# Gated linear attention and a maxout feed-forward: two groups of tokens ahead of most of the weight rounding

## The chip, the cores and the metric

The kernel runs on one core of a Trainium2 chip. The metric is the device time of one execution in microseconds. The core's engines work side by side, each through its own list of instructions in order: TensorE (PE, with its weight loads PEld), VectorE (DVE), ScalarE (ACT), GpSimd (POOL), and SyncE (SP), which here issues nearly all of the transfers.

## The reference

Inputs are q, k, v and a complex gate a for 4 batches, 8 heads, 768 positions and 48 channels, and four weight matrices of the feed-forward, which are 64-bit floating-point numbers (`randn(...).astype(float32)` times a 64-bit scalar).

```python
scale = np.minimum(mag, 0.999) / (mag + 1e-06)     # mag = |a|; a_n = a * scale
for t in range(S):                                 # state: 48 x 48, complex
    S_re, S_im = ar * S_re - ai * S_im + kv, ar * S_im + ai * S_re
    y[:, :, t] = np.einsum('bhd,bhde->bhe', q[:, :, t], S_re)
x = y.transpose(0, 2, 1, 3).reshape(3072, 384)
h = np.maximum(np.maximum(x @ w1, x @ w2), x @ w3) # 384 -> 768
out = h @ w_out                                    # 768 -> 384
```

## The kernel before

**Tiles and groups.** The 3072 tokens are 24 tiles of 128 (index x); two neighbouring tiles make a group (index g, 12 groups), and a batch is three groups. The recurrence is computed in chunks: inside a tile by masked score matrices, between tiles by a state G.

**A group's preparation** (`pre_steps`): three gate steps s0 to s2 (`gate_steps`: magnitude, logarithm, phase; most on ScalarE, which has to keep the order of its table functions, `tab`), the cumulated sums and exponentials (`products` part 0, matmuls "sums"), `angles` (arctangent, cumulated angles by the matmuls "cs", rounding t and nf, sine and cosine CS), and the turned operands uk and uq (`products` part 1). The work tiles L, w and e of the gates have one buffer each; ar and ai have two.

**A tile's steps** (`tile_steps`): scores A and B on TensorE (`scores`), their masked copies into atm on VectorE (`gather`, L554), the transposes of the next tile's operands (`turn`, "tp", copied to K and Q), its decay factors (`cut`, tile f), its scaled copies Q, KB, QB, QG (`prep`, L507), the state (`state`, "dk" and g), and the outputs (`outputs`, "y", copied to xT). Q and K have two buffers, KB, QB and QG one.

**The feed-forward** (`ffn_steps`): up steps, each for a few of the six 128-row blocks f and one of the three weights w1 to w3 (`up_step`; the first of three is copied to hT by ScalarE, L647, the others are joined by a maximum on VectorE, L649), then an output step for each tile (`out_step`). Tiles 0 and 1 go through it one by one, 128 tokens each; from group 1 on a whole group goes, 256 tokens.

**The weights** are read as 64-bit words and rounded to 32 bits on the chip, in twelve blocks: nine of w1 to w3 (blocks 0 to 2 hold the first third of the columns of w1, w2 and w3, and so on) and three of w_out. `weight_load` (L286) brings a block's raw words, `weight_round` (L303) rounds them: on VectorE L313, L315, L318, L320 and L321, on ScalarE L314 and L319, with a temporary tile ex of two buffers.

**Order.** The program is written step by step; a scheduler then orders each engine's list by readiness and by the place in the program, so a ready instruction may run well ahead of where it is written. `weave` merges lists of steps by a begin and an end fraction. Before the main loop stand the startup (group 0's gates, rounds 0 to 2, angles), then one `weave`: tiles 0 and 1, with the rounds and loads of blocks 3 to 11 spread over its first 0.7, the preparation of group 1 in 0.15 to 0.58, and tile 0's feed-forward in 0.4 to 0.8. The main loop `group(g)` follows for g from 1 to 11: two tiles' attention, the preparation of group g + 1, the first two gate steps of g + 2 (`later`), and the feed-forward of the tokens before, handed out by `feed`; one output step is held over to the next group. From group 2 on TensorE's list is fixed in program order (`T["chain"]`).

Of the kernel before, what the change touches and what calls it, by code (L numbers as in the profile page):

```python
# [9 lines left out]
FP = mybir.dt.float32  # L10
# [38 lines left out]
def kernel(  # L49
# [31 lines left out]

    C8, C8B, C16, C32, CK, CG, CD, NF = 0, 4, 8, 12, 20, 28, 36, 37
    HC = DM // 2
    MAGIC = 12582912.0
    LNMAX = math.log(0.999)
    TWOPI = 6.283185
# [199 lines left out]
    def weight_load(i):  # L286

        dst, src = blocks[i]
        if src.dtype == FP:
            nc.sync.dma_start(out=dst, in_=src)  # L290
            return
        n, m = dst.shape[1:]
        if i in (0, 1, 2, 6):
            room = (ws[1], ws[2], wo)[i % 4].rearrange("p f m -> p (f m)")
            room = room[:, FF // 3 * KD:].rearrange("p (n m) -> p n m", n=n)
        elif i == 5:
            room = un2.tile([P, n, 2 * m], FP, tag="Q", name="raw")
        else:
            room = fp2.tile([P, n, 2 * m], FP, tag="hT", name="raw")
        T["raw", i] = room.bitcast(I32)  # L300
        nc.sync.dma_start(out=T["raw", i], in_=src.bitcast(I32))

    def weight_round(i):  # L303

        dst, src = blocks[i]
        if src.dtype == FP:
            return
        n, m = dst.shape[1:]
        raw = T["raw", i].rearrange("p n (m w) -> p n m w", w=2)
        low, high = raw[:, :, :, 0].bitcast(U32), raw[:, :, :, 1]  # L310

        ex = fp2.tile([P, n, m], I32, tag="xT", name="ex")
        nc.vector.tensor_scalar(out=ex, in0=high, scalar1=0x7FF00000, scalar2=None, op0=OP.bitwise_and)  # L313
        nc.scalar.activation(out=ex, in_=ex, func=AF.Relu, scale=8.0, bias=wbias)  # L314
        nc.vector.scalar_tensor_tensor(out=ex, in0=high, scalar=-0x80000000, in1=ex,  # L315
                                       op0=OP.bitwise_and, op1=OP.bitwise_or)
# [292 lines left out]
    def outputs(x, xs):  # L609

        atm, V, G, QG = T["atm", x], T["v", x], T["G", x], T["QG", x]
        y = banks("y", DM).rearrange("p (k t) -> p k t", k=KD)
        queues = [[] for _ in range(4)]
        for r in range(DM // 32):
            i, w = divmod(r, 3)
            runs = ((0,), (1, 2), (3,))[w]
            for c in range(2):
                todo = [(n, new) for new in (True, False) for n in runs]
                queues[r % 4] += [(r, c, i, n, new, (n, new) == todo[0], (n, new) == todo[-1]) for n, new in todo]
        for todo in zip(*queues):  # L620
            for r, c, i, n, new, start, stop in todo:
                (j, h), lo = divmod(2 * i + n // 2, 4), 32 * n
                mm(out=y[32 * (r % 4):32 * (r % 4) + 32, r // 4, c * L64:(c + 1) * L64],
                                 lhsT=V[:, c, i, lo:lo + 32] if new else G[0:DD, c, i, lo:lo + 32],
                                 rhs=atm[:, 4 * c + h] if new else QG[0:DD, 2 * (4 * c + h) + j], start=start, stop=stop)
        if x == xs[0]:

            T["xT", xs[-1]] = fp2.tile([P, KD, P], FP, tag="ot", name="xT") if len(xs) == 1 else \
                fp2.tile([P, KD, TG], FP, tag="xT", name="xT")
        o = (x - xs[0]) * P  # L630
        nc.scalar.copy(out=T["xT", xs[-1]][:, :, o:o + P], in_=y)


    def up_step(xs, fs, i):
        xT, n = T["xT", xs[-1]], len(xs) * P
        if fs[0] == 0 and i == 0:

            T["hT", xs[-1]] = ld2.tile([P, KF, n], FP, tag="ar", name="hT") if xs[0] == 0 else \
                fp2.tile([P, KF, n], FP, tag="hT", padded_shape=[P, KF, TG], name="hT")
        dst = T["hT", xs[-1]][:, fs[0]:fs[-1] + 1]  # L640
        ps = banks("up", len(fs) * n).rearrange("p (f t) -> p f t", t=n)
        for j, f in enumerate(fs):
            for d in range(KD):
                mm(out=ps[:, j], lhsT=ws[i][:, d, f * P:(f + 1) * P], rhs=xT[:, d],
                                 start=(d == 0), stop=(d == KD - 1))
        if i == 0:
            nc.scalar.copy(out=dst, in_=ps)  # L647
        else:
            nc.vector.tensor_tensor(out=dst, in0=dst, in1=ps, op=OP.max)  # L649
# [20 lines left out]

    def tokens(x):

        return [x] if x < C else [x // C * C + c for c in range(C)]

    def ffn_steps(xs):

        n = 2 if xs[0] == 0 else 3
        return [call(up_step, xs, range(f, f + n), i) for f in range(0, KF, n) for i in range(3)] \
            + [call(out_step, xs, x) for x in xs]

    def front(x):
# [21 lines left out]
    weight_load(2)  # L703
    load_kq(0, 1)
    load(0, load_v)
    for i in range(3, 6):
        weight_load(i)
    for t in fs:
        nc.gpsimd.memset(t[L64 // 2:L64], 0.0)
    for t in gs:  # L710
# [6 lines left out]
            f()  # L717
    for c in range(C):
        products(c)[0]()
    for i in range(3):  # L720
        weight_round(i)
# [22 lines left out]
    def group(g):  # L744
        x, y = g * C, g * C + 1
        load(g + 1, load_v)
        load(g + 2, load_a, load_kq)
        ffn = held + ffn_steps(tokens(x - 1))
        held[:] = [ffn.pop()]

        def feed(n):
            for _ in range(min(n, len(ffn))):
                ffn.pop(0)()

        pre = pre_steps(g + 1, feed) if g + 1 < NG else [lambda: None] * 8
        gates, sums, (turning,), units = pre[:3], pre[3:5], pre[5:6], pre[6:]
        later = gate_steps(g + 2, list(range(C)))[:2] if g + 2 < NG else []

        def pairs(x):
            for f in (scores, gather):  # L760
                for nm in "AB":
                    f(x, nm)

        def turned(x):

            if x < NX:
                turn(x, "k")
# [73 lines left out]
```

## Time and profile before

| | us |
|---|---|
| median of 3 runs | 715.44 (714.9 to 716.07) |
| the profiled execution | 714.05 |
| its span, first to last instruction | 712.3 |
| TensorE busy in the span | 631.8 (89%) |
| VectorE busy | 510.0 (72%) |
| ScalarE busy | 388.6 (55%) |
| GpSimd busy | 119.1 (17%) |

The page cuts the span into 40 slices of some 17.8 us and gives each engine's busy tenths, with the clock granted to TensorE in tenths of full speed. A table of windows gives the busy time in chosen stretches. A group row gives engine, operation, tiles and shape, the count, the summed busy time and the mean of one in ns, then the engine's idle time just before, and what ended it. A row of waits reads: who waited for whom, us in total, times, the longest. A row of the timeline begins with its start and its length in us.

### The profile page before, as it was taken

The numbers are of one execution on the slowest core, as the hardware profiler recorded it, in microseconds if no ns is written. First come the engines' busy times: TensorE is split into PE (matmuls) and PEld (weight loads), VectorE is DVE, ScalarE is ACT, GpSimd is POOL, SyncE is SP. The second block draws the span as 40 slices with busy tenths as digits, with TensorE's granted clock in tenths as the row PEclk, the third lists the DMA queues.
The fourth block names the chain that finished last, engine by engine and source line by source line (L and its number), as shares of the span: only waits on it lengthen the run. The fifth ranks groups of instructions, "written<-read, shape, count | busy, mean of one in ns | idle before, by whom it ended". The sixth has DMA issues, their size and how long they took to land.

```text
span 712.3 us, 25175 instructions
## 1 busy us (share of the span) xinstructions
PE 631.8 (89%) x11196; PEld 517.9 (73%) x11196; DVE 510.0 (72%) x695; ACT 388.6 (55%) x617; POOL 119.1 (17%) x121
## 2 busy tenths in 40 slices
PE   1246497688899999999999999999999999999997
PEld 0144385576787887888878878878878878877785
DVE  5899899777767777787786787768687678556111
ACT  6678564746575485476476466466655654520010
POOL 9300400501301301302213013013013023000000
PEclk9967799879999999999999999999999999999999
DMA  8455552032042141231330330320420120000000
GB/s 212 130 146 132 126 136 47 12 65 51 18 75 47 21 76 43 37 69 34 57 59 24 58 64 19 70 56 13 80 59 14 29 52 3 2 25 3 13 12 23
DMA packets 138285, 39.41 MB, mean 55 GB/s; under 512 B 130880, under 2 KB 133952, under 8 KB 138176
## 3 DMA queue, kind: packets, MB, share of 16 engines
q1 hardware_dynamic: 137664, 37.78, 24.3%
q8 instruction: 88, 1.44, 0.9%
q14 instruction: 21, 0.17, 0.1%
q10 hardware_dynamic: 512, 0.01, 0.0%
HBM read 33.03 MB, written 4.72 MB: 53 GB/s over the span
## 4 chain that ended last, share of the span: by engine, by line
PE 56%; ACT 16%; DVE 12%; issue 10%; SPq 3%; POOL 1%; ACTq 1%; DMA 1%; POOLq 0%
PE up L114 27%; PE op L114 12%; PE cs L114 5%; DVE Q L507 3%; PE y L114 3%; DVE KB L507 3%; PE B L114 3%; ACT f L109 3%; PE tp L114 3%; ACT K L476 2%; ACT CS L109 2%; PE dk L114 2%; PE A L114 2%; ACT Q L480 2%; ACT e L109 2%
## 5 line engine op out<-in xcount | busy, mean ns | idle before, releaser
L114 PE MATMUL up<-xT,w 128*128 128x256 f32 (+1 forms) x1404 | 295.3, 368 | 2.7 <-ACT f L109 0.7
L114 PEld LDWEIGHTS up<-xT,w 128*128 128x128 f32 x1404 | 248.4, 191 | 40.2 <-ACT f L109 3.6
L114 PE MATMUL op<-wo,hT 128*128 128x384 f32 x288 | 100.7, 500 | 1.0 <-DVE wo L321 0.5
L647 ACT COPY hT<-up 128x768 f32<-128x768 f32 (+2 forms) x27 | 19.6, 726 | 120.0 <-PE up L114 119.7
L114 PEld LDWEIGHTS op<-wo,hT 128*128 128x128 f32 x288 | 53.3, 191 | 35.1 <-DVE wo L321 0.9
L367 POOL TENSOR_TENSOR ai<-ai,L 128x768 f32<-128x768 f32 x10 | 24.3, 2426 | 322.0 <-ACT L L109 265.0
L649 DVE TENSOR_TENSOR hT<-hT,up 128x768 f32<-128x768 f32 (+2 forms) x54 | 46.4, 860 | 42.7 <-PE up L114 42.6
L507 DVE TENSOR_TENSOR Q<-Q,f 112x512 f32<-112x512 f32 x48 | 40.8, 851 | 42.8 <-ACT f L109 42.7
L507 DVE TENSOR_TENSOR QB<-Q,f 112x512 f32<-112x512 f32 (+1 forms) x48 | 57.4, 1232 | 0.0
L114 PE MATMUL cs<-w,upto 128*64 128x192 f32 x192 | 31.0, 381 | 29.4 <-DVE w L385 29.4
L114 PE MATMUL y<-atm,vb 128*32 128x64 f32 x1536 | 47.5, 224 | 0.0
L114 PE MATMUL y<-QG,g 112*32 112x64 f32 x1536 | 46.9, 222 | 0.2 <-issue 0.2
L114 PEld LDWEIGHTS y<-atm,vb 128*32 128x32 f32 x1536 | 39.8, 112 | 9.9 <-ACT ar L371 3.3
L114 PEld LDWEIGHTS cs<-w,upto 128*64 128x64 f32 x192 | 19.0, 156 | 36.6 <-issue 19.5
L398 DVE SCALAR_TENSOR_TENSOR nf<-t,cs 128x384 f32<-128x384 f32 x24 | 13.3, 554 | 39.9 <-ACT t L396 39.9
L114 PEld LDWEIGHTS y<-QG,g 112*32 112x32 f32 x1536 | 40.3, 112 | 0.9 <-DVE g L606 0.5
L109 ACT ACTIVATE f<-F 48x296 f32<-48x296 f32 x96 | 39.6, 412 | 0.8
L507 DVE TENSOR_TENSOR KB<-K,f 112x1024 f32<-112x1024 f32 x24 | 37.3, 1553 | 0.0
L114 PE MATMUL sums<-Ln,mid 64*64 64x192 f32 x192 | 15.0, 363 | 25.1 <-DVE Ln L357 23.8
L464 DVE TENSOR_TENSOR uk<-uk,En 128x768 f32<-128x768 f32 x24 | 23.0, 957 | 19.2 <-PE tp L114 19.2
L454 POOL TENSOR_TENSOR k<-E,k 128x384 f32<-128x384 f32 x20 | 23.7, 1186 | 76.6 <-ACT E L109 76.6
L114 PE MATMUL B<-QB,KB 112*32 112x80 f32 x1536 | 32.6, 237 | 2.5 <-DVE QB L507 2.2
(111 smaller groups left out, 1071.5 us busy)
## 6 DMA issues: line engine op xcount, KB each, us to landing
ar<-in_a_re_dram SPq DMA_DIRECT2D x24, 192.0 KB, 3.3
ai<-in_a_im_dram SPq DMA_DIRECT2D x24, 192.0 KB, 3.8
k<-in_k_dram SPq DMA_DIRECT2D x96, 48.0 KB, 2.6
q<-in_q_dram SPq DMA_DIRECT2D x96, 48.0 KB, 2.4
vb<-in_v_dram SPq DMA_DIRECT2D x192, 24.0 KB, 2.2
out_dram<-ot SPq DMA_DIRECT2D x24, 192.0 KB, 2.4
raw<-in_moe_w_dram SPq DMA_DIRECT2D x5, 768.0 KB, 5.5
raw<-in_moe_w_out_dram SPq DMA_DIRECT2D x3, 768.0 KB, 4.8
```

Of the source, the lines that this page charges most:

```text
L109: tab(nc.scalar.activation(**kw))
L114: ins = f(**kw)
L367: (nc.gpsimd if g > 1 else nc.vector).tensor_tensor(out=ai, in0=ai, in1=L, op=OP.mult)
L398: nc.vector.scalar_tensor_tensor(out=nf, in0=t, scalar=MAGIC, in1=ps, op0=OP.subtract, op1=OP.subtract)
L454: eng.tensor_tensor(out=hd(T[nm, x]), in0=E, in1=hd(T[nm, x]), op=OP.mult)
L464: nc.vector.tensor_tensor(out=u, in0=u, in1=two(T["En", x]), op=OP.mult)
L476: nc.scalar.copy(out=T["K", x][0:DD], in_=src)
L480: nc.scalar.copy(out=T["Q", x][0:DD, :, 0:32], in_=src.rearrange("p s (a t) -> p (s a) t", a=4))
L507: nc.vector.tensor_tensor(out=out, in0=in_, in1=f.to_broadcast([DD, 2 * H, n, 8]), op=OP.mult)
L647: nc.scalar.copy(out=dst, in_=ps)
L649: nc.vector.tensor_tensor(out=dst, in0=dst, in1=ps, op=OP.max)
```

## The change

The rounding of blocks 3 to 11 leaves the first `weave`. Tiles 0 and 1 go with the preparation of group 1 alone. A second `weave` takes tiles 2 and 3, the preparation of group 2, the round of block 3 and the first three up steps of group 0, which is now a group of 256 tokens. Then come blocks 4 to 11: each is rounded, and the up steps of groups 0 and 1 that need it follow. In it tile 4's transposes and `prep` are written behind the last round. The main loop starts at group 2 (FIRST), with what is left: four up steps of group 1 and the four output steps of both groups, and all three gate steps of group 3.

Buffers move too: raw blocks 0 to 2 lie in the part of their own weight tile that is not yet used, block 3 in wo, and blocks 4 to 11 take turns in two buffers of Q and the one of QB. The temporary ex lies in wo for blocks 0 to 3 (one place), later in the gates' w and e by turns. Group 1's gate inputs are loaded in the startup, ahead of the raws.

```diff
@@ weight_load, weight_round @@
-        if i in (0, 1, 2, 6):
-            room = (ws[1], ws[2], wo)[i % 4].rearrange("p f m -> p (f m)")
-            room = room[:, FF // 3 * KD:].rearrange("p (n m) -> p n m", n=n)
-        elif i == 5:
+        if i < 3:
+            room = ws[i][:, :, FF // 3:]
+        elif i == 3:
+            room = wo.rearrange("p f m -> p (f m)")[:, 0:2 * n * m].rearrange("p (n m) -> p n m", n=n)
+        elif i % 3 == 0:
+            room = un1.tile([P, n, 2 * m], FP, tag="QB", name="raw")
+        else:
             room = un2.tile([P, n, 2 * m], FP, tag="Q", name="raw")
-        else:
-            room = fp2.tile([P, n, 2 * m], FP, tag="hT", name="raw")
...
-        ex = fp2.tile([P, n, m], I32, tag="xT", name="ex")
+        if i < 4:
+            ex = wo.rearrange("p f m -> p (f m)")[:, 2 * n * m:].rearrange("p (n m) -> p n m", n=n).bitcast(I32)
+        else:
+            ex = nat1.tile([P, n, m], I32, tag="we"[i % 2], name="ex")
@@ tokens, ffn_steps, tile_steps @@
-        return [x] if x < C else [x // C * C + c for c in range(C)]
+        return [x // C * C + c for c in range(C)]
...
-        n = 2 if xs[0] == 0 else 3
+        n = 2 if xs[0] < FIRST * C else 3
...
-        tr, ct, pr = front(x + 1)
-        kt = [products(x + 1)[2]] if x + 1 < NX else []
+        tr, ct, pr = front(x + 1) if x + 1 < FIRST * C else ([], [], [])
+        kt = [products(x + 1)[2]] if x + 1 < FIRST * C else []
@@ startup and weaves @@
-    for i in range(3, 6):
-        weight_load(i)
+    load(1, load_a)
...
-    weight_load(6)
-    load(1, load_a)
...
-    rounds = []
-    for i in range(3, len(blocks)):
-        rounds.append(call(weight_round, i))
-        if i + 4 < len(blocks):
-            rounds.append(call(weight_load, i + 4))
-    load(1, load_v, load_kq)
-    ffn = ffn_steps([0])
-    weave((0.0, 1.0, tile_steps(0) + tile_steps(1)), (0.0, 0.7, rounds), (0.15, 0.58, pre_steps(1)),
-          (0.4, 0.7, ffn[:9]), (0.72, 0.8, ffn[9:]))
+    load(1, load_kq, load_v)
+    weight_load(3)
+    weave((0.0, 1.0, tile_steps(0) + tile_steps(1)), (0.15, 0.58, pre_steps(1)))
     load(2, load_a, load_kq)
+    load(2, load_v)
+    ffns = [ffn_steps(tokens(g * C)) for g in range(FIRST)]
+    weave((0.0, 1.0, tile_steps(2) + tile_steps(3)), (0.15, 0.75, pre_steps(2)), (0.0, 0.7, rounds[3:4]),
+          (0.5, 1.0, ffns[0][:3]))
+    for i in range(4, 7):
+        weight_load(i)
+    for f in ffns[0][3:4] + ffns[1][:2]:
+        f()
+    for i in range(4, len(blocks)):
+        rounds[i]()
+        if i + 3 < len(blocks):
+            weight_load(i + 3)
+        for f in ffns[0][i:i + 1] + ffns[1][i - 2:i - 1] if i < 7 else ffns[0][i:i + 1] if i < 9 else []:
+            f()
+    x = FIRST * C
+    for f in sum(front(x), []) + [products(x)[2]]:
+        f()
+    ffns = ffns[1][5:7] + ffns[0][9:] + ffns[1][7:]
@@ group, main loop @@
         load(g + 1, load_v)
+        if g == FIRST:
+            load(g + 1, load_a, load_kq)
         load(g + 2, load_a, load_kq)
-        ffn = held + ffn_steps(tokens(x - 1))
+        ffn = held + ffn_steps(tokens(x - 1)) if g > FIRST else ffns
...
-        if g > 1:
-            feed(1)
+        feed(1)
         pairs(x)
-        for f in gates if g == 1 else gates[2:]:
+        for f in gates if g == FIRST else gates[2:]:
...
-    for g in range(1, NG):
-        if g == 2:
-            T["chain"] = None
+    T["chain"] = None
+    for g in range(FIRST, NG):
         group(g)
```

More of the change, by code (lines that the diff above doesn't have):

```diff
@@ L83 @@
     HC = DM // 2
+    FIRST = 2
     MAGIC = 12582912.0
@@ L626, in outputs @@
         if x == xs[0]:
-            T["xT", xs[-1]] = fp2.tile([P, KD, P], FP, tag="ot", name="xT") if len(xs) == 1 else \
-                fp2.tile([P, KD, TG], FP, tag="xT", name="xT")
+            T["xT", xs[-1]] = fp2.tile([P, KD, TG], FP, tag="xT", name="xT")
         o = (x - xs[0]) * P
@@ L636, in up_step @@
         if fs[0] == 0 and i == 0:
-            T["hT", xs[-1]] = ld2.tile([P, KF, n], FP, tag="ar", name="hT") if xs[0] == 0 else \
-                fp2.tile([P, KF, n], FP, tag="hT", padded_shape=[P, KF, TG], name="hT")
+            T["hT", xs[-1]] = fp2.tile([P, KF, n], FP, tag="hT", name="hT")
         dst = T["hT", xs[-1]][:, fs[0]:fs[-1] + 1]
@@ L719 @@
         products(c)[0]()
+    rounds = [call(weight_round, i) for i in range(len(blocks))]
     for i in range(3):
-        weight_round(i)
-    weight_load(6)
-    load(1, load_a)
+        rounds[i]()
     angles(0, list(range(C)))
@@ L727 @@
         f()
-    rounds = []
-    for i in range(3, len(blocks)):
-        rounds.append(call(weight_round, i))
-        if i + 4 < len(blocks):
-            rounds.append(call(weight_load, i + 4))
-    load(1, load_v, load_kq)
-    ffn = ffn_steps([0])
-    weave((0.0, 1.0, tile_steps(0) + tile_steps(1)), (0.0, 0.7, rounds), (0.15, 0.58, pre_steps(1)),
-          (0.4, 0.7, ffn[:9]), (0.72, 0.8, ffn[9:]))
-    load(2, load_a, load_kq)
+    load(1, load_kq, load_v)
+    weight_load(3)
+    weave((0.0, 1.0, tile_steps(0) + tile_steps(1)), (0.15, 0.58, pre_steps(1)))
+    load(2, load_a, load_kq)
+    load(2, load_v)
[7 more added lines that the diff above has]
+    for i in range(4, len(blocks)):
+        rounds[i]()
+        if i + 3 < len(blocks):
[6 more added lines that the diff above has]
+    ffns = ffns[1][5:7] + ffns[0][9:] + ffns[1][7:]
     held = []
```

## The prediction

> **What bounds the kernel now.** I read the slices of the page first: they tell where TensorE stops waiting.
>
> ```profile
> PE   1246497688899999999999999999999999999997
> DVE  5899899777767777787786787768687678556111
> PEclk9967799879999999999999999999999999999999
> ```
>
> From the twelfth slice (about 200 us) TensorE is full at full clock; before it VectorE is full and TensorE idles, with a lowered clock. So the change, which touches only the front, is worth what it does to the time at which the full stretch is reached. As milestones I take the first masked copy of a tile's scores, which VectorE's timeline shows at 52.46 (tile 0), 117.54 (tile 2), 170.41 (4), 224.60 (6) and 276.31 us (8). The busy table cut there has, in its columns, the stretch, its length, then busy us (and instructions) of PE, PEld, DVE, ACT, POOL, the granted clock, DMA share, GB/s:
>
> ```profile
> 0.00:52.46 52.46, 14.51 (x196) 11.30 (x200) 41.29 (x80) 35.92 (x62) 22.25 (x60) 0.90 0.65 165
> 52.46:117.54 65.08, 44.75 (x930) 36.66 (x926) 62.20 (x95) 41.16 (x62) 7.13 (x1) 0.82 0.46 112
> 117.54:170.41 52.87, 41.48 (x939) 35.11 (x933) 39.67 (x55) 34.33 (x54) 9.73 (x6) 0.87 0.25 49
> 170.41:224.60 54.19, 51.25 (x929) 41.60 (x922) 41.82 (x52) 33.01 (x51) 10.93 (x8) 1.00 0.24 47
> 224.60:276.31 51.71, 51.53 (x957) 42.33 (x947) 39.11 (x52) 30.66 (x50) 9.13 (x6) 1.00 0.25 49
> ```
>
> Call them stages S0 to S4. S1 is VectorE's: 62.2 of 65.1 us busy, since rounding fills every gap of the attention. S2 is nobody's: VectorE 75% busy, TensorE 78% at clock 0.87. Its waits show a chain instead:
>
> ```profile
> ACT t L396 <- PE cs L114: 9.4, 2, 6.0
> PE cs L114 <- DVE w L385: 6.6, 1, 6.6
> DVE nf L398 <- ACT t L396: 5.1, 2, 3.3
> ```
>
> The next group's gates, angles and turns pass from engine to engine, and the next tile's scores need them. S3 and S4 are TensorE's. From tile 8 on its order is fixed and the same in both kernels, and its backlog is too, so the shift of tile 8's milestone is the shift of the end.
>
> The prices of a rounding and of the feed-forward (groups by shape, then TensorE's timeline):
>
> ```profile
> L313 DVE TENSOR_SCALAR ex<-raw 128x768 int32<-128x768 int32 x8 | 4.4, 556 | 0.2 <-DMA raw<-in_moe_w_out_dram 0.2
> L315 DVE SCALAR_TENSOR_TENSOR ex<-raw,ex 128x768 int32<-128x768 int32 x8 | 7.6, 953 | 0.7 <-ACT ex L314 0.7
> L649 DVE TENSOR_TENSOR hT<-hT,up 128x256 f32<-128x256 f32 x6 | 2.5, 421 | 0.5 <-PE up L114 0.5
> L649 DVE TENSOR_TENSOR hT<-hT,up 128x384 f32<-128x384 f32 x4 | 2.2, 545 | 0.0
> ```
>
> ```profile
> 31.45 2.18 PE L114 MATMUL cs<-w,upto 128*64 128x192 f32 x10 [13.21 <-DVE w L385]
> ...
> 188.90 8.04 PE L114 MATMUL up<-xT,w 128*128 128x256 f32 x36
> 196.87 1.19 PE L114 MATMUL cs<-w,upto 128*64 128x192 f32 x10
> ...
> 213.05 4.14 PE L114 MATMUL op<-wo,hT 128*128 128x384 f32 x12
> ```
>
> A round is two VectorE instructions of 0.56 (L313, L318) and three of 0.95 us (L315, L320, L321): 3.97 us, and 3.5 net, as neighbours in the timeline overlap by about 0.09 each. ScalarE adds 0.93 + 0.92. An up matmul over 256 tokens costs 8.04/36 = 0.22 us, an output step of 12 matmuls 4.1 us. The same ten cs matmuls take 2.18 us cold and 1.19 warm.
>
> **What the skill says.** "TensorE: Matmul & The Clock Gate", "Part 1: The HAM clock gate", has an idle array at half clock and frees it after some 3.4 us of activity; the trace agrees (2.18 against 1.19 us). Its "Architectural detail" says that VectorE and ScalarE are strict FIFO, so a late operand holds all behind it; the waits above fit. "SBUF — State Buffer", "Who interferes with whom", has VectorE and GpSimd exclude each other on a shared port pair; the trace fits: GpSimd's one-row carry subtraction (L375) took 7.13 us beside busy VectorE at 74 us and 1.31 us at 135 us. "Perfetto Trace Analysis", "Optimization Strategy", advises interleaving regimes with different limits; before does that in S1, after does it later.
>
> **The change, part by part.**
>
> *Startup (S0).* Raws 3 to 5 leave SP's queue, so group 1's gates load there at once: in before their four issues took 9.3 us (31.5 to 40.9) behind three raws of 768 KB. ScalarE loses three rounding steps between the angles and the first exponentials (36.8 to 44.7 us, 2.5 us in all). The temporary ex of rounds 0 to 3 is now one buffer: a round starts only after the one ahead, for round 2 at 26.4 instead of 20.2 us; VectorE idles 3.4 us of 20 to 37.5, which holds most of that. I take a gain of 1.5 us (between 0 and 2.5): tile 0 at 51.
>
> *Tiles 0 and 1 (S1).* What goes: rounds 3 to 11, whose VectorE instructions in S1 sum to 29.8 us, 26.4 net, and six maxima of 0.42. 62.2 - 26.4 - 2.5 = 33.3 us are left; round 3 may run into the gaps (instructions do run far ahead of where they are written: ScalarE squared group 2's ai at 78.5 us), so 36.8 us is the floor. The bound is the chain. S2 shows it: from the gates' Ln at 119.95 us to tile 4's masked copy 50.5 us. Here Ln(1) can start when tile 0's exponentials end, 5 us ahead of the milestone, and group 1's ai product is VectorE's 0.95 instead of GpSimd's 2.6 us: 50.5 - 5 - 1.6 = 44 us, where before has 65.1. Ends: 38 (the floor) and 50.
>
> *Tiles 2 and 3, and eight rounds (S2).* S2's 39.7 us of VectorE lose tile 1's maxima (2.2) and the early gates of the group after next (L346, L347, L357: 2.5), which move on by a stage: 35.0. Added are 8 x 3.5 = 28.2 for the rounds, and nine maxima of 128x512 (0.42 + 2 x 0.125 = 0.67, an estimate from the two forms; net 0.6): 5.4. Sum 68.6. How full can VectorE be? Raws 4 and 5 take tile 2's and 3's Q buffers, raw 6 QB. Even rounds' ex takes the gates' w, free only when the angles' matmuls of group 2 have read it; in S2 those ended 33 us into the stage. Afterwards come nearly all eight rounds, tile 4's preparation (Q, Q, KB, QB, QG, uk: 6.6) and some 5 us of maxima: 40 us, 42 at 95%. So 33 + 42 = 75 us; and 68.6 us at 88%, between the 95% of S1 and the 75% of S2, are 78. I take 76.5; 72 if rounds run ahead, 84 if VectorE is only 82% busy. Hidden work: SP issues 36 loads of 0.62 for group 2 and eight raws; a raw lands in 4.8 us and has two rounds (7 us) of time; if one is late VectorE waits up to 5 us. ScalarE: 34 + 8 x 1.85 = 49 us of 76. TensorE: a steady group is 51.5 - 108 x 0.22 - 2 x 4.1 = 19.5 us of attention; 14 up steps of 12 x 0.22 = 2.65 make 37; together 57 us at full clock.
>
> *Group 2 (S3).* All its three gate steps come inside, as in group 1 of before, so the chain of S2 returns: 52.9 us, though TensorE has only 19.5 + 4 x 2.65 + 3 x 4.1 = 42 us, against 51.3 in before's S3. The saved feed-forward therefore isn't all turned to time. I take 53 (warm cs takes off 2 us, the fuller TensorE gives it back); bounds 44 and 57.
>
> *Group 3 (S4).* It follows a chain-bound group, as before's S3 did: 54.2 instead of 51.7. Then all is equal. The edits of xT, hT and of the wait-free first feed cost nothing: 256 tokens take one matmul where 128 took two of half length (4.29 us for 36), and the copies are as long in sum.
>
> Sum: 51 + 44 + 76.5 + 53 + 54.2 = 278.7, against 276.3: +2.4 us on a profiled execution of 714.05 us (span 712.3 and 1.75 around it), so 716.5. The median shown is 715.44: **718 us** with the same step.
>
> **The rivals.** *Group 2 is bound by throughput, and it ends faster.* In S2 of before the chain ran on a TensorE at 0.87; after eleven up steps it is warm and has work queued, so the stage could take what the engines need: 42 to 44 us. Then 718 - 9 = 709; it decides when the stage is under 49 us (-1.4 overall). For it: S3 of before holds the same chain under 51 us of TensorE. Against it: there two gate steps had been done ahead.
>
> *TensorE cold in the long stage, and it ends slower.* The 57 us fit 76.5 only above a clock of 0.74. Weight blocks come one per 4 to 5 us and feed 2.65 or 5.3 us of matmuls; at 0.65, as in the slices at 60 us, they need 87 us, +11: 729. For it: clock 0.74 at 140 to 160 us with TensorE 73% busy. Against it: 0.91 at 100 to 140.
>
> *Nothing moves.* If the long stage takes 74 us, the gain in S1 is just given back: 715.4.
>
> **How the numbers follow.** About 0.2% (1.4 us) can be told from no change. The forecast (its own range 712 to 724: S1 from 40 to 48 us or S2 from 72 to 80) has 0.48: 0.06 faster, 0.12 same, that is the third rival, 0.30 slower. Throughput-bound group 2, with or without a better filled S2, 0.27, reaching to 703. Cold TensorE, or VectorE at 82%, 0.25, reaching to 737. So faster 0.33, same 0.12, slower 0.55; cutting a tenth or less at each side leaves 706 to 734.
>
> **What would show it.** Tile 0's masked copy at 50 to 52, tile 2's at 91 to 99, tile 4's at 167 to 179, tile 6's near 225. Between tile 2 and tile 4 VectorE should be over 85% busy and the clock over 0.75. S3 above 50 us, with waits of cs for w and of nf for t as in S2, would carry the chain; S3 near 44 is the first rival. The prediction fails if the rounds start well before group 2's angles (a shorter S2), or if raws hold SP's queue and the gates of group 2 or 3 load late.

## The result, and the profile after

The changed kernel takes 726.67 us (median of 4 runs, 725.24 to 727.43) against 715.37 for the kernel before: a ratio of 1.0155, 95% interval 1.0135 to 1.0174. It is slower by some 11 us: on the forecast's side, but 8.7 us above its number of 718. That lies inside the whole range of 706 to 734 and above the 712 to 724 of the main forecast, where the prediction had set its rivals for a slower end; and it did not come about by the sum that the forecast drew up. The profiled execution has a span of 725.5 us against 712.3, so there are 13.2 us to find.

Lines of the code after the change are numbered 2 higher in `weight_load` and 5 higher from the round's instructions on: the round's L313 to L321 are L318 to L326, the gates' L346 is L351, w before the angles L385 is L390, the masked copy L554 is L559.

The slices of the page, three rows of section 2:

```profile
PE   0255363989898999999999999999999999999997
DVE  5775798699787778777766777787786787656111
PEclk9967587899999999999999999999999999999999
```

TensorE's row is lower than before in slices 5 to 7 (some 73 to 127 us: 3, 6, 3 where before has 4, 9, 7), and so is its clock (5, 8, 7 where before has 7, 9, 9). The table of busy time by stages, cut at the first masked copies of tiles 0, 2, 4, 6 and 8 (columns: stretch, length, busy us of PE, PEld, DVE, ACT, POOL, granted clock, DMA share, GB/s):

```profile
0.00:52.99 52.99, 14.71 (x196) 11.38 (x200) 37.70 (x72) 33.18 (x58) 19.53 (x60) 0.88 0.51 113
52.99:105.77 52.78, 26.80 (x816) 22.63 (x812) 39.64 (x59) 33.78 (x51) 3.77 (x1) 0.73 0.36 71
105.77:188.51 82.74, 63.87 (x989) 54.04 (x984) 70.41 (x97) 44.30 (x65) 9.68 (x6) 0.89 0.40 105
188.51:238.31 49.80, 46.48 (x907) 34.99 (x900) 40.05 (x52) 33.69 (x54) 11.79 (x7) 0.98 0.26 54
238.31:288.95 50.64, 49.45 (x919) 40.52 (x918) 39.19 (x51) 31.45 (x50) 9.27 (x7) 1.00 0.25 49
```

Tile 8's milestone moved from 276.31 to 288.95, by 12.6 us; from there to the end it is 436.0 us before and 436.6 after. So the front holds nearly all of it. TensorE's work up to there is about equal (203.5 us before, 201.3 after). Its idle time, stage length less busy time, isn't:

| TensorE idle, us | S0 | S1 | S2 | S3 | S4 | sum |
|---|---|---|---|---|---|---|
| before | 38.0 | 20.3 | 11.4 | 2.9 | 0.2 | 72.8 |
| after | 38.3 | 26.0 | 18.9 | 3.3 | 1.2 | 87.6 |

Of the added 14.9 us, 13.1 stand in S1 and S2. Three places in the trace show how.

**The gates of group 1 start late.** VectorE's timeline of the changed kernel, rows of 47 to 56 us:

```profile
47.77 0.69 DVE L512 TENSOR_TENSOR Q<-Q,f 112x512 f32<-112x512 f32 x1 [1.95 <-ACT f L110]
...
51.86 1.22 DVE L512 TENSOR_TENSOR QG<-Q,f 112x1024 f32<-112x1024 f32 x1
52.99 0.72 DVE L559 COPY_PREDICATED atm<-maskd,A 128x512 f32<-128x512 uint8 x1
53.61 0.94 DVE L351 TENSOR_TENSOR L<-L,w 128x768 f32<-128x768 f32 x1
54.47 0.43 DVE L559 COPY_PREDICATED atm<-masko,A 128x256 f32<-128x256 uint8 x1
54.80 0.55 DVE L352 TENSOR_SCALAR L<-L 128x768 f32<-128x768 f32 x1
```

The squares that L351 adds were done on ScalarE by 48.6 us (L350 at 47.77, for 0.84). L351 runs 5 us later: in VectorE's list all of tile 0's scaled copies and its masked copy stand ahead of it.

**Block 3 lands late.** VectorE's timeline again, then the DMA queue's own (start, length, how many):

```profile
61.22 0.96 DVE L362 SCALAR_TENSOR_TENSOR Ln<-L,e 128x768 f32<-128x768 f32 x1 [2.20 <-ACT L L361]
67.41 0.56 DVE L318 TENSOR_SCALAR wo<-wo 128x768 int32<-128x768 int32 x1 [5.23 <-DMA wo<-in_moe_w_dram]
67.88 0.69 DVE L512 TENSOR_TENSOR Q<-Q,f 112x512 f32<-112x512 f32 x1
68.48 1.22 DVE L512 TENSOR_TENSOR KB<-K,f 112x1024 f32<-112x1024 f32 x1
69.62 0.95 DVE L368 TENSOR_TENSOR w<-w,e 128x768 f32<-128x768 f32 x1
```

```profile
52.64 9.98 SPq L266 DMA_DIRECT2D vb<-in_v_dram  x12
62.67 0.59 SPq L303 DMA_DIRECT2D wo<-in_moe_w_dram  x1
```

Block 3's load is written behind all of group 1's loads, so SP issues it at 62.67. Its first rounding instruction had already been reached in VectorE's list, and holds tile 1's Q and KB and the gates' L368 for 5.2 us.

**The feed-forward piles up.** The chain of work up to tile 4's scores, in order of time:

```profile
128.32 4.89 PE cs L115 x24
...
137.60 6.16 DMA raw<-in_moe_w_dram
...
143.79 0.56 DVE ex L318
...
148.21 0.47 DVE g L612
...
148.73 1.67 PE y L115 x104
150.41 27.82 PE up L115 x128
178.23 0.89 PE tp L115 x8
179.14 0.89 ACT K L481
...
185.12 1.75 DVE QB L512 x2
```

Ahead of the cs, TensorE sat idle for 13.3 us; tile 3's scores, whose operands were there, stood behind. Afterwards it has 128 up matmuls in one stretch of 27.8 us, and only behind them tile 4's transposes and the copies that its scores need. The start of that stretch hangs on the late rounds as well: VectorE waits 1.96 us for a raw block at 143.79, tile 3's state (g) stands behind that instruction, and y waits for g. The raw is late because SP issues its load at 137.60, behind a load of k (136.90) that waits for VectorE's uk (135.91). The same stage in pieces (columns as above):

```profile
105.77:133.13 27.36, 13.78 (x328) 10.97 (x320) 20.56 (x25) 14.30 (x23) 9.68 (x6) 0.70 0.35 76
133.13:150.34 17.21, 14.78 (x362) 12.07 (x361) 14.47 (x24) 8.74 (x14) 0.00 (x0) 1.00 0.58 160
150.34:178.07 27.73, 27.73 (x136) 24.37 (x130) 25.99 (x38) 13.68 (x18) 0.00 (x0) 1.00 0.49 138
178.07:188.51 10.44, 7.58 (x174) 6.63 (x176) 9.39 (x12) 7.58 (x11) 0.00 (x0) 0.93 0.01 2
```

For 27 us TensorE is half empty at clock 0.70; for the 55 that follow it works 50.1 us at full clock or near it (0.93 to 1.00), and VectorE 49.9. In the first 133 us it has worked 55.3 us, in the kernel before 72.5: 17 us of TensorE's work were moved behind that point, where there is little room for them.

### The profile page after: what moved, and what is told of

It is laid out like the page before. It is cut to its first block, busy times and chain, and to the rows that moved or that the text cites. A ratio compares the mean times of both kernels' runs of the same rounds, so it can differ in the third digit from the quotient of the medians.

```text
span 725.5 us, 24955 instructions
## 1 busy us (share of the span) xinstructions
PE 629.7 (87%) x11088; PEld 514.6 (71%) x11088; DVE 512.9 (71%) x693; ACT 390.0 (54%) x616; POOL 114.0 (16%) x121
## 4 chain that ended last, share of the span: by engine, by line
PE 59%; DVE 13%; issue 11%; ACT 11%; SPq 3%; DMA 1%; POOL 1%; ACTq 0%; POOLq 0%; DVEq 0%
PE up L115 31%; PE op L115 12%; PE cs L115 4%; DVE Q L512 3%; PE y L115 3%; PE B L115 3%; PE tp L115 3%; DVE KB L512 3%; ACT f L110 3%; ACT K L481 2%; PE A L115 2%; ACT Q L485 2%; DVE g L611 2%; SPq L256 1%; PE dk L115 1%
## 5 line engine op out<-in xcount | busy, mean ns | idle before, releaser
L115 PE MATMUL up<-xT,w 128*128 128x256 f32 x1296 | 292.7, 383 | 0.8
L115 PEld LDWEIGHTS up<-xT,w 128*128 128x128 f32 x1296 | 243.0, 190 | 39.8 <-ACT f L110 2.6
L115 PE MATMUL op<-wo,hT 128*128 128x384 f32 x288 | 98.7, 493 | 2.0 <-DVE hT L650 1.3
L115 PEld LDWEIGHTS op<-wo,hT 128*128 128x128 f32 x288 | 53.1, 190 | 36.7 <-DVE hT L650 1.9
L648 ACT COPY hT<-up 128x768 f32<-128x768 f32 (+1 forms) x26 | 19.5, 749 | 110.5 <-PE up L115 110.3
L650 DVE TENSOR_TENSOR hT<-hT,up 128x768 f32<-128x768 f32 (+1 forms) x52 | 46.0, 884 | 42.0 <-PE up L115 42.0
L115 PEld LDWEIGHTS cs<-w,upto 128*64 128x64 f32 x192 | 19.2, 156 | 49.7 <-issue 32.5
L115 PEld LDWEIGHTS y<-atm,vb 128*32 128x32 f32 x1536 | 39.6, 112 | 10.5 <-issue 3.7
L403 DVE SCALAR_TENSOR_TENSOR nf<-t,cs 128x384 f32<-128x384 f32 x24 | 13.3, 554 | 38.0 <-ACT t L401 38.0
L115 PE MATMUL B<-QB,KB 112*32 112x80 f32 x1536 | 34.1, 244 | 4.2 <-DVE QB L512 4.0
L459 POOL TENSOR_TENSOR k<-E,k 128x384 f32<-128x384 f32 x20 | 25.2, 1259 | 69.8 <-ACT E L110 66.1
L115 PEld LDWEIGHTS B<-QB,KB 112*32 112x32 f32 x1536 | 30.0, 116 | 5.3 <-issue 3.1
```

The costliest lines, as they stand in the source:

```text
L115: ins = f(**kw)
L403: nc.vector.scalar_tensor_tensor(out=nf, in0=t, scalar=MAGIC, in1=ps, op0=OP.subtract, op1=OP.subtract)
L459: eng.tensor_tensor(out=hd(T[nm, x]), in0=E, in1=hd(T[nm, x]), op=OP.mult)
```

## The experiments

The theory after the first look: *TensorE's work decides. The first stage is a chain of one group's preparation whatever runs beside it; before, tile 0's feed-forward and nine roundings were done under it for nothing. Taken out, they are length elsewhere.* The rivals: *the late rounds decide* (VectorE's work, or w, which they hold, in the long stage), and *single waits decide* (block 3's load; the one temporary of the startup; the order of angles and ups). Ratios are to the kernel before, run beside each; stages in us.

| | ratio, 95% interval | S0 | S1 | S2 | S3 | S4 | tile 8 |
|---|---|---|---|---|---|---|---|
| before | 1 | 52.5 | 65.1 | 52.9 | 54.2 | 51.7 | 276.3 |
| changed kernel | 1.0155 (1.0135 to 1.0174) | 53.0 | 52.8 | 82.7 | 49.8 | 50.6 | 289.0 |
| before, tile 0's feed-forward later | 1.0131 (1.0087 to 1.0176) | 53.8 | 65.6 | 64.6 | 51.5 | 52.9 | 288.3 |
| block 3 early | 1.0097 (1.0064 to 1.0129) | 52.8 | 49.5 | 83.5 | 49.5 | 50.9 | 286.2 |
| two temporaries | 1.0095 (1.0059 to 1.0130) | 53.1 | 49.4 | 84.3 | 49.0 | 50.7 | 286.6 |
| temporary not in w | 1.0158 (1.0106 to 1.0211) | 52.6 | 54.2 | 81.1 | 49.8 | 50.6 | 288.3 |
| angles later | 1.0233 (1.0203 to 1.0263) | 52.9 | 54.5 | 85.8 | 49.5 | 50.6 | 293.3 |
| rounds 3 to 5 early | 1.0178 (1.0143 to 1.0212) | 52.5 | 51.5 | 84.9 | 49.7 | 50.4 | 289.1 |
| ups before the angles | 1.0132 (1.0110 to 1.0155) | 52.6 | 54.7 | 78.8 | 49.8 | 50.9 | 286.7 |
| four ups later | 1.0366 (1.0341 to 1.0391) | 52.6 | 54.6 | 77.7 | 66.5 | 53.0 | 304.3 |
| block 3 early, ups before | 1.0082 (1.0067 to 1.0097) | 52.9 | 50.9 | 78.7 | 49.7 | 50.7 | 282.9 |
| these and both temporaries | 1.0065 (1.0045 to 1.0084) | 53.6 | 46.6 | 81.6 | 49.0 | 49.7 | 280.5 |
| tile 4 before the last ups | 1.0193 (1.0169 to 1.0216) | 52.9 | 51.6 | 79.9 | 55.2 | 50.4 | 290.1 |
| all of it | 1.0127 (1.0098 to 1.0157) | 53.8 | 47.6 | 82.6 | 53.6 | 49.7 | 287.2 |

Each stage is read from one execution. Five of these runs leave the first stage's code as the changed kernel has it (temporary not in w, angles later, ups before the angles, four ups later, tile 4 before the last ups), and its length there is 51.6 to 54.7 us: a difference of a stage below some 3 us tells little by itself.

### One part alone, on the kernel before

```diff
-    ffn = ffn_steps([0])
     weave((0.0, 1.0, tile_steps(0) + tile_steps(1)), (0.0, 0.7, rounds), (0.15, 0.58, pre_steps(1)),
-          (0.4, 0.7, ffn[:9]), (0.72, 0.8, ffn[9:]))
+          )
...
-        ffn = held + ffn_steps(tokens(x - 1))
+        ffn = held + (ffn_steps([0]) if g == 1 else []) + ffn_steps(tokens(x - 1))
```

Tile 0's h also lies in the common buffer for it, and its ups take three blocks of rows each. The rounds stay where they were.

> The kernel before, with one thing alone: tile 0's feed-forward (17 us of TensorE, a maximum for each up step) leaves the first weave and is handed out with tile 1's in group 1; the rounds stay in the first weave. Theory A (TensorE work taken out of the first stage is work that its idle time no longer hides; it comes back as length of the next stage): the first stage gets at most 3 us shorter (VectorE still rounds through it, some 59 us of work), the next one 7 to 12 us longer, since it has only 11 us of idle TensorE and its chain; ratio to before 1.007 to 1.014. Theory B (what the change lost is in its late rounds and their buffers; TensorE's work has room in the second stage): first stage 2 to 3 us shorter, second up to 3 us longer, ratio 0.997 to 1.003.

Measured: 1.0131, the first stage not shorter at all (+0.5), the second 11.7 us longer. The table of busy time for these two stages:

```profile
53.79:119.34 65.55, 30.15 (x804) 25.75 (x800) 60.36 (x89) 39.75 (x58) 7.14 (x1) 0.66 0.50 117
119.34:183.90 64.56, 54.50 (x1028) 47.60 (x1021) 45.11 (x62) 39.83 (x62) 12.29 (x7) 0.92 0.19 36
```

TensorE idles 35.4 us in the first stage, 15.1 more than before, and to tile 8 the idle sum is 85.7 us, 12.9 more; tile 8 comes 12.0 later. Theory A holds: TensorE is busy 14.6 us less in the first stage, which VectorE paces and which is no shorter for it, and 13.0 us more in the next, which is longer by most of that. That is nearly the idle time that the changed kernel adds (14.9 us) and its delay at tile 8 (12.6), from one of its parts alone. It shows that this part can cost so much, not that the changed kernel's loss is the same one: there the first stage did get shorter, by 12.3 us, and single waits make up a part (below). (The moved work has one place in this run; a better one might cost less.)

### Single waits of the first stage

Block 3's load right behind group 1's gate loads in the startup:

```diff
     load(1, load_a)
+    weight_load(3)
...
     load(1, load_kq, load_v)
-    weight_load(3)
```

> The raw of block 3 is asked for in the startup, behind group 1's gate inputs, and not behind group 1's k, q and v. Theory A (VectorE stood 5.2 us at 62.2 us for this raw, with the gates of group 1 behind it, on the chain): tile 2's masked copy comes 5 to 6 us earlier than 105.8 us and the whole is 4 to 6 us faster than the changed kernel, ratio to before about 1.007 to 1.010. Rival B (the long stage with eight rounds sets the time whatever goes ahead of it): tile 2 comes earlier but tile 4's masked copy stays at 188 us, ratio 1.0155. Rival C (the other idle of that stage is latency, which takes the place of the wait): tile 2 no earlier than 104 us.

The wait is gone (the load is issued at 32.96) and the first stage is 3.2 us shorter; the ratio falls by 0.006, some 4 us. A real cause, for about a third of the loss.

Rounds 0 to 2 with two temporaries in the buffer of xT, as before:

```diff
-        if i < 4:
+        if i < 3:
+            ex = fp2.tile([P, n, m], I32, tag="xT", name="ex")
+        elif i < 4:
```

> The temporary of rounds 0 to 2 has two buffers again, in the place of the changed kernel's single one. Theory A (single-buffered rounds push the angles of group 0 back): the first cs matmul goes from 33.05 us back to about 31.4 us, tile 0's masked copy from 53.0 to about 51 us, and the whole 1.5 to 2 us faster, ratio about 1.013. Rival (the startup waits for inputs or table functions, and the temporary is hidden): first cs at 33 us and ratio 1.0155.

The startup got no shorter (tile 0 at 53.13, the first cs at 32.69), so the single temporary isn't what the startup lost. Yet the first stage lost 3.4 us. VectorE's timeline of this kernel (two lines further down in the code) tells why:

```profile
45.44 0.96 DVE L353 TENSOR_TENSOR L<-L,w 128x768 f32<-128x768 f32 x1 [0.37 <-ACT L L352]
...
57.72 0.95 DVE L370 TENSOR_TENSOR w<-w,e 128x768 f32<-128x768 f32 x1
...
66.19 0.56 DVE L320 TENSOR_SCALAR wo<-wo 128x768 int32<-128x768 int32 x1 [5.54 <-DMA wo<-in_moe_w_dram]
```

ScalarE's timeline:

```profile
47.91 0.84 ACT L110 ACTIVATE L<-L 128x768 f32<-128x768 f32 x1
...
66.78 0.94 ACT L321 ACTIVATE wo<-wo,biases 128x768 int32<-128x768 int32 x1 [4.55 <-DVE wo L320]
67.62 0.83 ACT L110 ACTIVATE L<-L 128x768 f32<-128x768 f32 x1
```

The first gate instruction on VectorE (L351 in the changed kernel, at 53.61) now stands ahead of tile 0's scaled copies, at 45.44, and the gates' Ln on ScalarE runs at 47.91 instead of 56.26. So this run removes the first of the three places, the late gates. The wait for block 3 is as long as ever, 5.54 us, and it holds the gates too: ScalarE's Exp (67.62; 71.48 in the changed kernel) stands behind the round's instruction, which waits 4.55 us for the same block. Of the 8.4 us at the head 3.4 are left at tile 2. The order changed by chance of the scheduler and wasn't set by itself. But the two edits do not remove one and the same cause: the run that has both, with two more edits of later parts (below), has a first stage of 46.6 us, shorter by 6.2, where 3.2 and 3.4 make 6.6.

### The late rounds

Rounds 3 to 5 in the first weave, their raws loaded in the startup, the ups left where they are:

```diff
-    weave((0.0, 1.0, tile_steps(0) + tile_steps(1)), (0.15, 0.58, pre_steps(1)))
+    weave((0.0, 1.0, tile_steps(0) + tile_steps(1)), (0.15, 0.58, pre_steps(1)), (0.0, 0.7, rounds[3:6]))
```

> Blocks 3, 4 and 5 are loaded in the startup (4 and 5 into hT's buffers, not yet used) and rounded in the first 0.7 of the first weave; six blocks are left for the later rounding. Theory A (what was lost is VectorE's idle time in the first weave, 13 us, which rounding filled in the kernel before): tile 2's masked copy at 100 to 106 us in spite of 7 us more work, tile 4's 10 to 13 us earlier than 188.5, ratio to before 0.997 to 1.002. Rival B (the chain of the first weave lengthens by what is added): tile 2 at 108 us or later, tile 4 at 184 or later, ratio 1.010 or more.

VectorE took 5.9 us more work in the first stage, and that stage was 1.3 us shorter still (block 3 is loaded early here too). The long stage lost 5.8 us of VectorE's work and became 2.2 us longer. Its pieces, and TensorE's timeline:

```profile
133.00:150.00 17.00, 13.82 (x353) 11.35 (x351) 10.65 (x17) 5.06 (x8) 0.00 (x0) 0.92 0.57 157
150.00:178.50 28.50, 28.50 (x133) 25.09 (x131) 21.78 (x30) 10.86 (x15) 0.00 (x0) 0.99 0.27 71
178.50:188.96 10.46, 7.60 (x190) 6.51 (x189) 7.46 (x9) 7.58 (x11) 0.00 (x0) 1.00 0.01 2
```

```profile
149.96 28.72 PE L115 MATMUL up<-xT,w 128*128 128x256 f32 x130
178.52 1.04 PE L115 MATMUL tp<-ident,uk 128*112 128x128 f32 x8
```

VectorE works 39.9 of the last 56.0 us instead of 49.9 of 55.4, TensorE 49.9 (50.1), and tile 4 comes at 188.96 (188.51). So the amount of rounding doesn't set this stage's end; from 150 us on TensorE's list does. When that list's ups can begin is another matter. VectorE's timeline of this run:

```profile
146.09 0.56 DVE L320 TENSOR_SCALAR ex<-raw 128x768 int32<-128x768 int32 x1 [3.55 <-DMA raw<-in_moe_w_dram]
146.57 0.55 DVE L614 TENSOR_TENSOR g<-g,dk 112x384 f32<-112x384 f32 x1
```

VectorE stands 3.55 us for a raw block, longer than in the changed kernel (1.96), with tile 3's state behind it, for which y and then the ups wait. What the stage would be with fewer rounds and without this wait wasn't tried; the late raws stay a rival for a few us.

The temporary of rounds 4 to 11 in ar and ai instead of w and e:

```diff
-            ex = nat1.tile([P, n, m], I32, tag="we"[i % 2], name="ex")
+            ex = ld2.tile([P, n, m], I32, tag=("ar", "ai")[i % 2], name="ex")
```

> The changed kernel with one thing else: the temporary of rounds 4 to 11 lies in the gates' input buffers ar and ai by turns instead of w and e. Theory A (w, held by the late rounds' temporary, delays the late rounds and group 3's gates): group 3's rotated gates step starts before 170 instead of 177 us, the late rounds start before group 2's angles have ended, the group 2 stage is 46 to 48 instead of 49.8 us or the long stage 2 to 4 us shorter; ratio to before 1.008 to 1.012. Theory B (the rounds are not what the long stage waits for, and group 3's gates have slack): stages 53, 52.8, 81 to 83.5, 49 to 50.5; ratio 1.014 to 1.017. Theory C (ar and ai are also what group 3's gates load into, so the load comes late in their place): the group 2 stage 51 us or more; ratio over 1.018.

1.0158, with stages near theory B's. Group 3's w is squared at 168.15 instead of 176.07, but VectorE's L351, which adds it, runs at 176.09 (177.03): its ai now comes late (ScalarE waits 1.3 us for that load at 174.9), and VectorE's list holds the rounds ahead of it. The hold on w is real in the waits; a cost of it doesn't show in the times.

### Order inside the long stage

Ups of group 0 in front of the angles of group 2:

```diff
-          (0.5, 1.0, ffns[0][:3]))
+          (0.49, 0.56, ffns[0][:3]))
```

> The first three up steps of group 0 are written at 0.49 to 0.56 of the second weave instead of 0.5 to 1.0, so that they stand ahead of the angles' matmuls in TensorE's list. Theory D (the long stage is bound by TensorE's list: it idles 13.3 us for the angles at 115 to 128 us, then has 28 us of up matmuls back to back from 150 to 178 us, with tile 4's transposes behind them; what is taken into the idle comes off the end): the run of up matmuls begins 5 to 8 us earlier than 150.3 us, tile 4's masked copy comes 4 to 8 us earlier than 188.5 us, the whole 4 to 8 us faster, ratio 1.004 to 1.010. Rival E (VectorE's rounds bind that stage: 70 of 83 us busy): tile 4's masked copy moves by less than 2 us, ratio 1.013 to 1.016.

The long stage is 4.0 us shorter. But the first one is 1.9 longer in this execution, so tile 4 comes 2.4 us earlier and the run of ups begins 3.3 us earlier (147.03), both short of theory D's ranges and above rival E's; the ratio is 0.002 lower, within the two intervals and within E's range. Three ups, 36 matmuls, now run at 114 to 125 us, in the idle time ahead of cs. No wait for a raw stands ahead of the ups here, so the gain need not be the order's alone.

The preparation of group 2 later, so that tile 3's scores go ahead of its cs:

```diff
-    weave((0.0, 1.0, tile_steps(2) + tile_steps(3)), (0.15, 0.75, pre_steps(2)), (0.0, 0.7, rounds[3:4]),
+    weave((0.0, 1.0, tile_steps(2) + tile_steps(3)), (0.35, 1.0, pre_steps(2)), (0.0, 0.7, rounds[3:4]),
```

> In the second weave the preparation of group 2 is written into 0.35 to 1.0 instead of 0.15 to 0.75, so that tile 3's scores stand ahead of the angles in TensorE's list. Theory A (TensorE idled 13.3 us for the angles with tile 3's scores, ready about 10 us earlier, behind them): tile 3's masked copy moves from 137.7 to about 125 us, VectorE's idle before the first late round shrinks, and the whole is 2 to 4 us faster, ratio 1.010 to 1.013. Rival (the even rounds need the gates' buffer, which the angles free; later angles start the rounds later): the first of the eight rounds moves from 133 us to 138 us or more and the whole is 0 to 4 us slower, ratio 1.0155 to 1.021.

Tile 3's masked copy came 10.8 us earlier (126.87 instead of 137.66), tile 4's 4.7 later: cs moved from 128.3 to 138.3 us, the run of ups to 152.2 (126 matmuls). Tile 3's place behind the cs was no loss: in this stage it pays to have cs early.

Four more ups handed to the main loop:

```diff
-        ... if i < 7 else ffns[0][i:i + 1] if i < 9 else []:
+        ... if i < 6 else ffns[0][i:i + 1] if i < 7 else []:
...
-    ffns = ffns[1][5:7] + ffns[0][9:] + ffns[1][7:]
+    ffns = ffns[0][7:9] + ffns[1][4:7] + ffns[0][9:] + ffns[1][7:]
```

> Four of the eleven up steps among the late rounds (the last two of group 0 and two of group 1) are handed to group 2's attention instead. Theory D (TensorE's list binds, with nothing to gain in sum): tile 4's masked copy comes 3 to 8 us earlier, the stage from tile 4 to tile 6 gets longer by about as much, since TensorE is nearly full there (46.5 of 49.8 us), and the whole stays within 3 us of the changed kernel, ratio 1.011 to 1.020. Rival E (rounds on VectorE bind the stage): tile 4's masked copy stays at 188 us and the whole gets slower by up to 10 us, ratio 1.020 to 1.029. Rival F (group 2 is bound by its chain and has room): tile 6 comes 5 us or more earlier, ratio 1.008 or less.

The run of ups is 92 matmuls long, 20.12 us, and tile 4 comes 3.7 us earlier, though 10.5 us of TensorE were taken out: its scores now wait 4.7 us for VectorE's Q, so both engines are near their limit there. Then group 2's stage is 16.7 us longer, which no theory had; its cs wait for w until 213.15 at a cold clock (2.15 us for ten). TensorE's list shows the rest: between that cs and tile 6's scores (at 250.40) stand 21.9 us of up and output steps, where the changed kernel has 11.3. The four ups pushed output steps behind the cs, and tile 6's scores stand behind those.

### Together

Block 3 early and ups before the angles:

> The early raw of block 3 and the three up steps ahead of the angles together. If the wait for the raw and TensorE's idle time are separate causes, their gains add: 1.0155 less 0.0058 less what the up steps alone bring, that is ratio 1.000 to 1.005. If they are one (what one saves is waited for by the other), the ratio is that of the better of the two.

The ratio falls by 0.0073, against 0.0058 + 0.0023 = 0.0081 for the two alone: that agrees with separate gains that add, though the second is no larger than the intervals, and it is less than was hoped.

These two with both temporaries changed as well:

> All edits together: early raw of block 3, two buffers for the temporary of rounds 0 to 2, the up steps ahead of the angles, and the late rounds' temporary in the buffers of ar and ai, so that the first late rounds need not wait for the angles to free w. Theory D: the last of these brings 0 to 3 us more, since TensorE's list binds and not the rounds; ratio 0.997 to 1.003. Rival E (rounds bind): the late rounds start 10 us or more before 133 us and the ratio falls to 0.990 to 0.996.

1.0065, the best of the changed kernels, and still slower than before. The first stage is 46.6 us, near the forecast's 44; the gates' Ln runs at 48.41, right behind tile 0's exponentials. The run of ups is there in full (132 matmuls, 29.51 us from 142.0), though the late rounds began at 119.5 instead of 133 us. So 0.0090 of the 0.0155 were order, buffers and single waits, which can be mended with the change left in. The rest, some 4 us, fits the TensorE work that left the first stage; but no run puts tile 0's feed-forward back into the changed kernel's first weave, so for this rest the cause is argued and not shown.

Tile 4's transposes and copies ahead of the last ups, with raws 6, 9 and 11 in QB and 7, 8 and 10 in Q; the three ups of group 1 in this loop are written two rounds later, so that four ups follow tile 4's steps:

```diff
         rounds[i]()
-        if i + 3 < len(blocks):
+        if i in (4, 5, 6):
             weight_load(i + 3)
+        elif i == 7:
...
+            for f in tr + ct + pr[:1]:
+                f()
+        elif i in (8, 9):
+            weight_load(i + 2)
...
-        for f in ffns[0][i:i + 1] + ffns[1][i - 2:i - 1] if i < 7 else ffns[0][i:i + 1] if i < 9 else []:
+        for f in ffns[0][i:i + 1] + (ffns[1][i - 4:i - 3] if i > 5 else []) if i < 9 else []:
```

> The changed kernel with one edit: tile 4's transposes, decay factors and first scaled copy are written ahead of the last four up steps of the late rounds instead of behind all of them (to free a Q buffer in time, blocks 9 and 11 go into QB's buffer and only 7, 8 and 10 into Q's). Theory D (in the changed kernel tile 4 stands behind 28 us of up matmuls in TensorE's list, and 10 us from its transposes to its masked copy follow them): TensorE has 10 us of matmuls to run beside those 10 us, the masked copy comes 4 to 8 us earlier than 188.5 us, and the whole is 3 to 8 us faster, ratio 1.004 to 1.011. Rival E (rounds on VectorE end at 180.8 us and bind tile 4 by its scaled copies): the masked copy comes at 186 us or later, ratio 1.012 or more.

Tile 4 came 4.1 us earlier, as theory D had it, but group 2's stage took 5.4 us longer, and the whole was no faster (1.0193). VectorE's timeline of this kernel:

```profile
184.39 0.72 DVE L559 COPY_PREDICATED atm<-maskd,A 128x512 f32<-128x512 uint8 x1
185.00 0.95 DVE L351 TENSOR_TENSOR L<-L,w 128x768 f32<-128x768 f32 x1
```

Group 3's gates now begin behind tile 4's masked copy at 185.00, not at 177.03, and its cs at 211.65 instead of 210.93. Tile 6 follows the cs of group 3, not tile 4.

All edits at once (those of the last two, the early ups now four, and block 3's round written into the first 0.2 of the second weave):

> All edits together: raw of block 3 early, two buffers for the first temporary, the late temporary in ar and ai, four up steps ahead of group 2's angles, and tile 4 ahead of the last four up steps. If theory D holds and the causes add, this takes 3 to 6 us off the run with all edits but the last (ratio 1.0065): 0.998 to 1.002, the kernel before made good again. If the rounds bind by then: 1.004 to 1.007.

1.0127, slower than without the move of tile 4 (1.0065). Group 2's stage is long again, 53.6 instead of 49.0, and tile 4 came no earlier this time (183.93 instead of 181.79).

## Why the prediction was right and wrong

Slower was right, and so was its ground: the gain of the first stage is given back, with something more, in the long one. The size was not: the milestones of tiles 0, 2, 4 and 6 all came later than the prediction had named for them. The sum of +2.4 us was wrong by 10.2 at tile 8: +2.0 in S0, +8.8 in S1, +6.2 in S2, less 3.2 and 3.6 in S3 and S4. That the total came no further off is in part luck, as the last two show.

**Startup, 51 against 52.99.** The step "I take a gain of 1.5 us" failed. The first cs came at 33.05 instead of 31.45, for w at 32.05 (30.45). The single temporary was suspected, and two of them changed nothing. The trace has VectorE waiting 1.75 us for GpSimd's mask at 28.95, ahead of w; before, such a wait of 2.01 us stood behind w, at 34.88. But with two temporaries it stands behind w again (2.01 us, at 36.12), and tile 0 came no earlier (53.13), so this isn't it either. The cause stays open.

**Tiles 0 and 1, 44 against 52.78.** The step that failed is "Ln(1) can start when tile 0's exponentials end, 5 us ahead of the milestone". ScalarE's Ln ran at 56.26, 8.5 us after the exponentials' end at 47.74: 0.84 for its square, then 5.0 until VectorE reached L351, 1.7 to L352's end, and 0.9 for a copy of K ahead of it on ScalarE. From Ln to tile 2's masked copy it then took 49.5 us, where the forecast had 50.5 - 1.6 = 48.9. The head was placed by when the operands are ready and not by the engine's list. The trace of before had it: L346 at 118.16, right behind the masked copy at 117.54. The Trainium skill's "TensorE: Matmul & The Clock Gate", "Architectural detail", which the prediction named for the strict order of these engines, applies to this as to the waits. That the 49.5 us are so near 48.9 is luck: inside them lies block 3's wait (3.2 of 5.2 us felt), which the prediction put at nothing in this stage; it had priced a late raw only among the eight of the long stage. With the head where the prediction put it and the wait gone ("these and both temporaries"), the stage took 46.6 us.

**Tiles 2 and 3, 76.5 against 82.74.** The amounts were about right: VectorE's work 70.4 (68.6), its share 85% (88%), and the start of the late rounds 27.5 us into the stage (33). The step that failed is "afterwards ... 42 at 95%": 55.3 us came after. Tile 3's masked copies and state, group 2's turned operands and group 3's first gate instructions come there too, some 10 us of VectorE that the list of forty left out. And the limit was the wrong one. "Together 57 us at full clock", held against the 76.5 us as a whole, took TensorE for covered. But 14 of the 64 us that it works lie in the first 27, and the other 50 fill the last 55; the run with rounds 3 to 5 early shows that these stay with 10 us less of VectorE's work. A sum over a stage hides that the work sits at its end.

**Group 2 and group 3, 53 and 54.2 against 49.80 and 50.64.** "The chain of S2 returns" was too long by 3 us: cs followed warm and unwaited (1.19 us for ten, at 210.93). Tile 6 does follow group 3's chain rather than tile 4 (the run with tile 4 ahead of the last ups shows it), but that chain starts at 177, inside the long stage. S4 shows nothing of it: TensorE works 49.5 of its 50.6 us. These two errors hid 6.8 us of the others.

**The rivals.** Throughput-bound group 2 (42 to 44 us) came a third of the way, at 49.8, just over the 49 that the prediction had set as its sign. Cold TensorE gave the nearest time, 729, for the wrong reason: the long stage had a clock of 0.89, and 0.70 only in its first 27 us; it was in S1, at 0.73, that TensorE was cold. The case that shared its chance, a long stage of 84 us with VectorE 82% busy, was near in length (82.7 us, 85%), and it too took VectorE for the limit. "Nothing moves" named the swap, not its price. Edits costed at nothing (256 tokens at once, the feed without its wait) show no cost in S4, 50.6 us against 51.7.

## What to carry to other kernels

Work that an engine does while something else sets the stage's length costs nothing there, and moving it away frees nothing: ask of each engine's work, per stretch and not per stage, where it will lie afterwards and whether that stretch has idle time for it. The start of a chain is where its first instruction stands in the engine's list, not where its operands are ready; look for the instruction that it follows in the trace. And a gain at one milestone counts only if the next milestone hangs on it.

## What the runs showed of the hardware

Beside a working GpSimd, some of VectorE's instructions with two inputs took longer: w (L374) 1.73 instead of 0.95 us at 115.62, Q 1.48 instead of 0.69 at 117.28, KB 2.01 instead of 1.22, the QB pair 2.62 instead of 1.82 at 122.02 and 3.43 at 203.04, g (L611) 1.35 instead of 0.55 at 206.39. Each was longer by about 0.8 us (the second pair twice), whatever its own length. The Trainium skill's "SBUF — State Buffer", "Who interferes with whom", has the shared port pair; the prediction had used it for GpSimd's side alone, where the carry subtraction took 3.77 us in the changed kernel and 7.13 before. (The 1.31 us at 135 us that it set against the 7.13 is no quiet case: VectorE was at work there too.) In S2 these five (Q twice) stand one behind the other on the chain to cs and lengthen it by 3.9 us. The kernel before has the like there, 3.5 us at 132 to 142, so this is hardly a part of the loss.
